# One-hots of Y for two buckets at once, eight of twelve one-hot rows on ScalarE, scaled tables and 120 columns in a graph tensor-product kernel

## The chip, the cores and the metric

The kernel runs on one core of a Trainium2 chip. The core has a matrix engine (TensorE: PE in the profile, its weight loads as PEld), an engine for elementwise work and reductions (VectorE, DVE), one for functions of single elements with a scale and a bias (ScalarE, ACT), a general engine (GpSimd, POOL), and SyncE (SP), which only issues transfers here. POOL also issues the indirect transfers, whose row numbers come from a tile. SBUF is the working memory of 128 partitions; PSUM takes the results of matmuls; HBM is the large memory. Each engine takes its instructions in the order of its own program, and semaphores order them between engines.

The metric is the device time of one execution in microseconds: 9987.23 us, the median of three runs (9973.58 to 9994.59).

## The reference

```python
N, deg, C, L, DE = 10000, 64, 64, 1, 4        # E = N * deg = 640000 edges, M = 4
R = _silu(edge_feat @ w_rad)                              # (E, C)
xs = x[src]                                               # (E, C, M)
tp = jnp.einsum('eci,ef,ifo->eco', xs, Y, cg)             # (E, C, M)
msg = R[:, :, None] * tp
agg = _segment_sum(msg.reshape(-1, C * M), dst, N).reshape(N, C, M)
return jnp.einsum('ncm,cd->ndm', agg, w_mix)
```

For each edge a row of 256 numbers of x is gathered, scaled per channel by R, combined with the edge's four numbers Y by a small tensor cg, summed over the edges with the same destination node, and mixed over the channels.

## The kernel before

**Sorting the edges.** The kernel sorts the edges by destination on the chip and then sums in each bucket of 32 nodes with matmuls. An edge travels as a row of W = 9 numbers: a tag (destination and source in one word), four of Y, four of edge_feat. The edges come in three parts (SPLIT). The first pass (`pass1`) sends a part's edges to NG = 20 groups of nodes; the second (`pass2`) sends a group's edges to its 15 or 16 buckets (297 + 16 = 313 buckets in all, 13 groups with 16 and 7 with 15). Both use `route`. A chunk is up to T tiles of 128 edges (T is 16 for the first pass of the first part, 24 elsewhere) and is handled as two pieces. For each tile, a matmul whose stationary operand is a one-hot of the row to which each edge goes (`onehots`, tile oh) and whose moving operand is the edges' words spread over slots (`spread`, tile X) puts the edges in place in PSUM (`move`, L585); `evict` copies the result to rt, and `store` (L604) writes it with an indirect transfer. The number of destination rows is Q = 120 in the first pass (20 groups with 6 rows each) and 128 in the second.

**One-hots.** In `onehots` DVE compares an iota with the row numbers for the first v rows of a piece (L569). ACT makes the last `self.act` rows: one Square for each row (L574, into the tile sq), which gives the squared distance, and one Relu over all of them (L575, from sq to oh), which turns 0 into 1 and the rest into 0. `act` is 3 in the first stage and 6 later; a full piece has 8 rows in the first stage and up to 12 later. In the first stage POOL makes the last `self.spare` = 3 tiles of X of each piece and DVE the rest (L557).

**Tables.** `tables` works out where each tile's edges start. Counts by a matmul (cnt), a copy out of PSUM on ACT into ps.cols (L437), a running sum on DVE with a floor `low` (L442), then the sums times B plus the bucket number (at, L456), split into two bf16 halves (sb, L458 and L459). From the totals n (L445) and a few small matmuls (prep, fo) come the row numbers of the stores; over and inc are repeated into ovr by two DVE copies (L471, L472). It is called 92 times: 6 + 26 for the first pass and 60 for the second.

**Messages.** `messages` goes over 939 units, one for each bucket and part, with 5 tiles of 128 edges in the first part and 6 in the others. At step k it runs, in four quarters, stages for units at some distance: `index` (8 ahead: source rows and destinations out of the tag), `gather` (5 ahead: one indirect transfer for each tile, on POOL, L866, into one of LG + 2 = 7 buffers xg), `fetch` (4 ahead: SP reads the sums of earlier parts back, L935, four buffers old), `turn` (2 ahead: a transpose on PE, L879), `sums` (0: 2 matmuls for each tile into the one PSUM buffer G, L921), `silu` (1 ahead: ACT, L892); `turned` (ACT, L884) and `spots` (1 ahead); `products` (1 ahead: DVE, x rows times R, L910) and `evict` (0: G plus old, on DVE, L950; in the first part a copy on ACT, L952); `radial` (2 ahead, PE, L889) and `full`. In `spots` DVE makes for one unit the one-hot of the node within the bucket (eq, in PSUM, L900) and multiplies it by the edge's four Y (S, L903, two buffers).

**Order.** In the first stage the first pass of the first part runs alone, with SP's order written out. After it `groups` weaves by hand the messages of a part with the second pass of the next group and the first pass of the next part; the orders of PE, DVE and ACT are those of the program, POOL's and SP's follow a planner. The last stage, from the third part's first message, has no first pass left in it.

## Time and profile before

| | |
|---|---|
| median of three runs | 9987.23 us |
| profiled execution | 9996.25 us, of which the span of the profile is 9994.5 us |
| granted TensorE clock, mean | 0.839 of full speed |
| transfers | 680358 packets, 1086.59 MB, 109 GB/s over the span |
| read from HBM, written | 855.28 MB, 222.79 MB |
| first gather of x rows of the three parts | 741.6, 3608.8 and 6861.4 us |
| last gather | 9849.1 us |

One execution is profiled. A row of a table of groups has the line of the kernel, the engine, the operation, the tiles out<-in with shapes and a count; behind the bar the busy time in us and the mean of one in ns; behind the second bar the engine's idle time just before these instructions and what ended it. "issue" means that the engine waited for nothing that the profile shows, "remote" that the releaser is not known. A row of a timeline begins with the start in us and the duration. The ends of matmuls are modelled.

### The profile page before, as it was taken

To read this page: it belongs to the slowest core of one execution; us is meant where nothing else is said; L and a number is where in the kernel's file an instruction comes from. 1 tells how busy PE (TensorE), PEld (TensorE's weight loads), DVE (VectorE), ACT (ScalarE), POOL (GpSimd) and SP (SyncE) were. 2 spreads that over 40 slices of the span, in tenths; PEclk is the share of its full clock that TensorE was granted. 3 is DMA by queue.
4 is the path that set the end of the run, shared out by engine and by line. 5 is a ranking of instruction groups with operands and counts; after the bars stand their busy time and mean duration, and the time that the engine had idled before them with its cause. 6 is when DMAs were issued, how large, how long until landed. Compare 5 with 4: busy or idle time off the path is not lost. (4 is left out here: it accounts for less than half of the span.)

```text
span 9994.5 us, 140280 instructions
## 1 busy us (share of the span) xinstructions
PE 7919.2 (79%) x49142; PEld 6708.4 (67%) x49142; DVE 6590.0 (66%) x11187; ACT 3711.5 (37%) x10488; POOL 5816.1 (58%) x6222
## 2 busy tenths in 40 slices
PE   7877888888887788888888888777778778787775
PEld 6766677777776667766666777666666666666654
DVE  7885777777775677777777777565555555555543
ACT  4763454445443343433333434222222222232210
POOL 3635555555556655665555566666666666666663
PEclk8987888888888888888888888878888888888887
DMA  6113333333333334443433444444333333333331
GB/s 238 43 38 102 108 103 99 105 103 101 105 104 107 107 107 118 117 122 110 117 110 111 116 119 115 125 120 121 109 108 112 110 107 109 110 110 108 111 109 55
DMA packets 680358, 1086.59 MB, mean 109 GB/s; under 512 B 255481, under 2 KB 484935, under 8 KB 673384
## 3 DMA queue, kind: packets, MB, share of 16 engines
q0 software_dynamic: 282224, 774.67, 27.5%
q1 hardware_dynamic: 396280, 295.24, 10.2%
q8 instruction: 390, 6.39, 0.3%
q10 hardware_dynamic: 1152, 7.74, 0.2%
q14 instruction: 312, 2.56, 0.1%
HBM read 855.28 MB, written 222.79 MB: 108 GB/s over the span
## 5 line engine op out<-in xcount | busy, mean ns | idle before, releaser
L866 POOL DMA_INDIRECT xg<-in_x_dram,sidx x5321 | 5079.1, 955 | 3288.4 <-issue 1397.8
L921 PE MATMUL G<-S,xg 128*128 128x128 f32 x21284 | 3159.1, 312 | 828.4 <-issue 323.0
L921 PEld LDWEIGHTS G<-S,xg 128*128 128x128 f32 x21284 | 3014.1, 226 | 933.6 <-issue 385.6
L585 PE MATMUL pr<-X,oh 128*128 128x81 f32 (+14 forms) x20530 | 2980.3, 303 | 670.5 <-issue 368.7
L585 PEld LDWEIGHTS pr<-X,oh 128*128 128x128 f32 x20530 | 2790.2, 211 | 871.4 <-issue 517.6
L910 DVE TENSOR_TENSOR xg<-xg,pre 128x1536 f32<-128x1536 f32 (+1 forms) x939 | 1557.2, 1658 | 457.2 <-ACT pre L892 318.1
L574 ACT ACTIVATE sq<-i,row 128x128 f32<-128x128 f32 x5322 | 1663.0, 391 | 18.9 <-DVE row L541 11.6
L557 DVE TENSOR_TENSOR X<-dv,Wt 128x2052 f32<-128x2052 f32 (+11 forms) x814 | 1336.8, 1642 | 453.6 <-remote 147.3
L892 ACT ACTIVATE pre<-pre 128x384 f32<-128x384 f32 (+1 forms) x939 | 430.2, 458 | 2918.9 <-remote 1284.2
L903 DVE TENSOR_TENSOR S<-dv,pay 128x768 f32<-128x768 f32 (+1 forms) x939 | 857.3, 913 | 232.9 <-remote 110.0
L889 PE MATMUL pre<-wr,sT 54*128 54x384 f32 (+1 forms) x1878 | 905.7, 564 | 86.5 <-ACT sT L884 47.3
L575 ACT ACTIVATE oh<-sq,ones 128x768 f32<-128x768 f32 (+1 forms) x1000 | 861.9, 862 | 102.0 <-PE pr L585 37.8
L950 DVE TENSOR_TENSOR Gs<-old,G 128x256 f32<-128x256 f32 x313 | 131.7, 421 | 1048.6 <-remote 536.6
L569 DVE TENSOR_TENSOR oh<-dv,row 128x768 f32<-128x768 f32 (+3 forms) x960 | 796.4, 833 | 8.4 <-PE pr L585 8.4
L524 ACT ACTIVATE pc<-pp 128x480 f32<-128x480 f32 (+8 forms) x500 | 234.9, 470 | 797.0 <-remote 210.1
L884 ACT ACTIVATE sT<-pre 54x128 f32<-54x128 f32 (+1 forms) x939 | 245.2, 261 | 579.8 <-remote 240.3
L889 PEld LDWEIGHTS pre<-wr,sT 54*128 54x128 f32 (+1 forms) x1878 | 302.6, 201 | 232.0 <-issue 97.5
L604 POOL DMA_INDIRECT grp<-rt,idx x240 | 277.0, 1154 | 305.7 <-ACT rt L595 119.6
L604 POOL DMA_INDIRECT bkt<-rt,idx x260 | 260.8, 1003 | 307.4 <-ACT rt L597 129.2
L879 PEld LDWEIGHTS pre<-ident,pay 128*54 128x54 f32 (+1 forms) x939 | 109.1, 116 | 481.3 <-issue 250.4
L950 DVE TENSOR_TENSOR Gp<-old,G 128x256 f32<-128x256 f32 x313 | 130.6, 417 | 449.3 <-remote 235.8
L879 PE MATMUL pre<-ident,pay 128*54 128x128 f32 (+1 forms) x939 | 293.2, 312 | 120.6 <-DVE xg L910 85.2
(259 smaller groups left out, 4791.5 us busy)
## 6 DMA issues: line engine op xcount, KB each, us to landing
xg<-in_x_dram,sidx POOLq DMA_INDIRECT x5321
sums<-Gp SPq DMA_DIRECT2D x626, 128.0 KB
old<-sums SPq DMA_DIRECT2D x626, 128.0 KB
bkt<-z SPq DMA_DIRECT2D x26, 1024.0 KB
grp<-z SPq DMA_DIRECT2D x16, 1024.0 KB
pay<-bkt SPq DMA_DIRECT2D x208, 54.0 KB
out_dram<-ot SPq DMA_DIRECT2D x69, 128.0 KB
grp<-z ACTq DMA_DIRECT2D x7, 1024.0 KB
```

The source lines that it names most:

```text
L557: eng.tensor_tensor(X[:, b:e], msk[:, b:e].unsqueeze(3).to_broadcast([P, e - b, w, W]), CH[c][1][:, a + b:a + e, :].unsqueeze(2).to_broadc ...
L569: nc.vector.tensor_tensor(oh[:, :v, :], self.v128.unsqueeze(1).to_broadcast([P, v, P]), row[:, a:a + v].unsqueeze(2).to_broadcast([P, v, P ...
L574: nc.scalar.activation(sq[:, u - v, :], self.i128, AF.Square, bias=row[:, a + u:a + u + 1], scale=-1.0)
L575: nc.scalar.activation(oh[:, v:m, :], sq[:, :m - v, :], AF.Relu, bias=self.ones[:, 0:1], scale=-2.0)
L585: nc.tensor.matmul(PR[c][:, ps.lo[t] * W:ps.hi[t] * W], oh[:, u, :], Xs[u], start=(t == 0), stop=(t == sizes[c] - 1), skip_group_check=True)
L604: nc.gpsimd.indirect_dma_start(out=ps.dst, out_offset=bass.IndirectOffsetOnAxis(ap=idx[:Q, i:i + 1], axis=0), in_=RT.pop(c), in_offset=None)
L866: nc.gpsimd.indirect_dma_start(out=xg[:, t, :], out_offset=None, in_=self.x, in_offset=bass.IndirectOffsetOnAxis(ap=si[:, u:u + 1], axis=0))
L889: nc.tensor.matmul(R, ST_.pop(k)[:ut * W], self.wr[:ut * W, :ut * 64], start=True, stop=True)
L892: nc.scalar.activation(RT[k], RT[k], AF.Silu)
L903: nc.vector.tensor_tensor(S[:, :ut], self.eq[:, :ut].unsqueeze(3).to_broadcast([P, ut, NB, 4]), pb[:, :, 1:5].unsqueeze(2).to_broadcast([P ...
L910: nc.vector.tensor_tensor(V, V, R.unsqueeze(3).to_broadcast([P, ut, 64, 4]), op=OP.mult)
L921: nc.tensor.matmul(G[:, h].rearrange("p n f -> p (n f)"), V[:, t, 32 * h:32 * h + 32, :].rearrange("p c i -> p (c i)"), S[:, t].rearrange( ...
```

## The change

- `pass_consts`: the floors `low` are multiplied by B and the bucket number is added once, at the start. In `tables` the counts leave PSUM with a scale of B. The running sum then is what `at` was: the scaling on DVE and the cast go, ACT copies the sums to sb in bf16, DVE subtracts as before. n is divided by B again, through an integer tile. The two copies into ovr move from DVE to ACT.
- `onehots`: oh is used with Q columns (120 in the first pass). ACT's squares are written into oh, and the Relu works in place; sq goes. `act` is 8 after the first stage. `move` writes Q rows.
- first stage: `spare` is 4: POOL makes four tiles of X of each piece.
- `pass1`: the tag's copy into the chunk (L707) moves from DVE to ACT.
- `spots`: every second bucket makes eq and S for two buckets in one instruction each; S has twice the size, still two buffers, and eq takes twice the place in PSUM. For that pay and dlc lie without gaps.
- `fetch`: 3 ahead and last in the step where it was 4 ahead and in the first quarter; three buffers old instead of four.

```diff
@@ pass_consts
+        for low in {id(p.low): p.low, id(p.last[0]): p.last[0]}.values():
+            low = low.rearrange("p (b t) -> p b t", b=B)
+            nc.vector.scalar_tensor_tensor(low, low, float(B), self.v128[:64, :B].unsqueeze(2).to_broadcast([64, B, T + 1]),
+                                           op0=OP.mult, op1=OP.add)
@@ tables
-        nc.scalar.activation(cols[:, :, 1:m + 1], cnt[:H, :m * B].rearrange("p (t b) -> p b t", b=B), AF.Copy)
+        nc.scalar.activation(cols[:, :, 1:m + 1], cnt[:H, :m * B].rearrange("p (t b) -> p b t", b=B), AF.Copy,
+                             scale=float(B))
...
-        n = w("n", B, 32)
-        nc.vector.tensor_copy(n[:N], sums[:N, :, m])
+        n, ni = w("n", B, 32), w("ni", B, 32, d=I32)
+        nc.vector.tensor_scalar(ni[:N], sums[:N, :, m], 1.0 / B, 0.5 / B - 0.5, op0=OP.mult, op1=OP.add)
+        nc.vector.tensor_copy(n[:N], ni[:N])
+        sb = wk.tile([H, ps.T * B], BF, name="sb", tag="sb" + ps.key, bufs=3)
+        tb = sb[:, :m * B].rearrange("p (t b) -> p b t", b=B)
+        nc.scalar.activation(tb, sums[:, :, :m], AF.Copy)
...
-        nc.vector.scalar_tensor_tensor(tb(at), sums[:, :, :m], float(B),
-                                       self.v128[:H, :B].unsqueeze(2).to_broadcast([H, B, m]), op0=OP.mult, op1=OP.add)
-        nc.vector.tensor_copy(sb[:, :m * B], at[:, :m * B])
-        nc.vector.tensor_tensor(sb[32:, :m * B], at[32:, :m * B], sb[32:, :m * B], op=OP.subtract)
+        nc.vector.tensor_tensor(tb[32:], sums[32:, :, :m], tb[32:], op=OP.subtract)
...
-        nc.vector.tensor_copy(two[:, 0], rep(over[:N, :B]))
-        nc.vector.tensor_copy(two[:, 1], rep(inc[:N]))
+        nc.scalar.activation(two[:, 0], rep(over[:N, :B]), AF.Copy)
+        nc.scalar.activation(two[:, 1], rep(inc[:N]), AF.Copy)
@@ onehots
-            oh = self.ph.tile([P, ps.H, P], F, name="oh", bufs=3)
+            oh = self.ph.tile([P, ps.H, P], F, name="oh", bufs=3)[:, :, :Q]
...
-            sq = self.ph.tile([P, self.act, P], F, name="sq", bufs=1)
             for u in range(v, m):
-                nc.scalar.activation(sq[:, u - v, :], self.i128, AF.Square, bias=row[:, a + u:a + u + 1], scale=-1.0)
-            nc.scalar.activation(oh[:, v:m, :], sq[:, :m - v, :], AF.Relu, bias=self.ones[:, 0:1], scale=-2.0)
+                nc.scalar.activation(oh[:, u], self.i128[:, :oh.shape[2]], AF.Square, bias=row[:, a + u:a + u + 1], scale=-1.0)
+            nc.scalar.activation(oh[:, v:m], oh[:, v:m], AF.Relu, bias=self.ones[:, 0:1], scale=-2.0)
@@ move
-                nc.tensor.matmul(PR[c][:, ps.lo[t] * W:ps.hi[t] * W], oh[:, u, :], Xs[u],
+                nc.tensor.matmul(PR[c][:Q, ps.lo[t] * W:ps.hi[t] * W], oh[:, u, :], Xs[u],
@@ pass1
-            nc.vector.tensor_copy(Wt[:, :m, 0].bitcast(I32), SB[b][:, o:o + m])
+            nc.scalar.activation(Wt[:, :m, 0], SB[b][:, o:o + m].bitcast(F), AF.Copy)
@@ messages
         def spots(k):
             g, j, s = units[k]
...
+            if j % 2:
+                return
+            ut = tiles(k)[1]
+            b = min(2, self.nb(g[1]) - j)
+            n = b * ut
+            pb = self.pay[g][:, j:j + b].rearrange("p b (t w) -> p (b t) w", w=W)
+            dl = IDX[g][1][:, j * ut:(j + b) * ut]
+            nc.vector.tensor_tensor(self.eq[:, :n], self.i32.unsqueeze(1).to_broadcast([P, n, NB]),
+                                    dl.unsqueeze(2).to_broadcast([P, n, NB]), op=OP.is_equal)
+            S = ph.tile([P, 2 * UT, NB, 4], F, name="S")
+            nc.vector.tensor_tensor(S[:, :n], self.eq[:, :n].unsqueeze(3).to_broadcast([P, n, NB, 4]),
+                                    pb[:, :, 1:5].unsqueeze(2).to_broadcast([P, n, NB, 4]), op=OP.mult)
+            for i in range(b):
+                SS[k + i] = S[:, i * ut:(i + 1) * ut]
...
-                OLD[g, j] = ph.tile([P, 2, 4, NB], F, name="old", bufs=4)
+                OLD[g, j] = ph.tile([P, 2, 4, NB], F, name="old", bufs=3)
...
-        quarters = (((index, LI), (gather, LG), (fetch, 4), (turn, 2), (sums, 0), (silu, 1)), ((turned, 2), (spots, 1)),
-                    ((products, 1), (evict, 0)), ((radial, 2), (full, -1)))
+        quarters = (((index, LI), (gather, LG), (turn, 2), (sums, 0), (silu, 1)), ((turned, 2), (spots, 1)),
+                    ((products, 1), (evict, 0)), ((radial, 2), (full, -1), (fetch, 3)))
@@ run
-            self.rt_bufs, self.ls, self.act, self.spare = 20, 10, 3, 3
+            self.rt_bufs, self.ls, self.act, self.spare = 20, 10, 3, 4
...
-            self.rt_bufs, self.ls, self.act, self.spare = 3, 4, 6, 0
+            self.rt_bufs, self.ls, self.act, self.spare = 3, 4, 8, 0
```

More of the change, by code (lines that the diff above doesn't have):

```diff
@@ L268, in consts @@
         self.vmsk = self.dv[:, P:]
-        self.eq = self.vmsk[:, :UT * NB].rearrange("p (t n) -> p t n", n=NB)
+        self.eq = self.vmsk[:, :2 * UT * NB].rearrange("p (t n) -> p t n", n=NB)
         d = iota("dif", [[1, P]], cm=-1, at=self.ph)
@@ L452, in tables @@
         nc.tensor.matmul(pre_p[0:1, 64:64 + B], self.ones[:N, 0:1], n[:N], start=True, stop=True)
-        at = wk.tile([64, ps.T * B], F, name="at", bufs=1)
-        sb = wk.tile([H, ps.T * B], BF, name="sb", tag="sb" + ps.key, bufs=3)
-        tb = lambda t: t[:, :m * B].rearrange("p (t b) -> p b t", b=B)
-        nc.vector.scalar_tensor_tensor(tb(at), sums[:, :, :m], float(B),
-                                       self.v128[:H, :B].unsqueeze(2).to_broadcast([H, B, m]), op0=OP.mult, op1=OP.add)
-        nc.vector.tensor_copy(sb[:, :m * B], at[:, :m * B])
-        nc.vector.tensor_tensor(sb[32:, :m * B], at[32:, :m * B], sb[32:, :m * B], op=OP.subtract)
+        nc.vector.tensor_tensor(tb[32:], sums[32:, :, :m], tb[32:], op=OP.subtract)
         yield
@@ L565, in onehots @@
             m = z - a
-            oh = self.ph.tile([P, ps.H, P], F, name="oh", bufs=3)
+            oh = self.ph.tile([P, ps.H, P], F, name="oh", bufs=3)[:, :, :Q]
             v = max(m - self.act, 0)
             if v:
-                nc.vector.tensor_tensor(oh[:, :v, :], self.v128.unsqueeze(1).to_broadcast([P, v, P]),
-                                        row[:, a:a + v].unsqueeze(2).to_broadcast([P, v, P]), op=OP.is_equal)
-            sq = self.ph.tile([P, self.act, P], F, name="sq", bufs=1)
+                nc.vector.tensor_tensor(oh[:, :v], self.v128[:, :Q].unsqueeze(1).to_broadcast([P, v, Q]),
+                                        row[:, a:a + v].unsqueeze(2).to_broadcast([P, v, Q]), op=OP.is_equal)
             for u in range(v, m):
-                nc.scalar.activation(sq[:, u - v, :], self.i128, AF.Square, bias=row[:, a + u:a + u + 1], scale=-1.0)
-            nc.scalar.activation(oh[:, v:m, :], sq[:, :m - v, :], AF.Relu, bias=self.ones[:, 0:1], scale=-2.0)
+                nc.scalar.activation(oh[:, u], self.i128[:, :oh.shape[2]], AF.Square, bias=row[:, a + u:a + u + 1], scale=-1.0)
+            nc.scalar.activation(oh[:, v:m], oh[:, v:m], AF.Relu, bias=self.ones[:, 0:1], scale=-2.0)
             XO[k][1] = oh
@@ L798, in pass2 @@
             n = sum(SPLIT[k][1])
-            pay = ph.tile([P, MB, max(sum(u) for _, u in SPLIT) * W], F, name="pay")[:, :, :n * W]
+            pay = ph.tile([P, MB * max(sum(u) for _, u in SPLIT) * W], F, name="pay")
+            pay = pay[:, :MB * n * W].rearrange("p (b q) -> p b q", b=MB)
             self.load_bucket(pay, k, g)
@@ L848, in index @@
             nc.vector.tensor_scalar(di[:, :m, :ut], key, 14, None, op0=OP.logical_shift_right)
-            dl = ph.tile([P, MB, MT], F, name="dlc", bufs=2)
+            dlc = ph.tile([P, MB * MT], F, name="dlc", bufs=2)[:, :m * ut]
+            dl = dlc.rearrange("p (b t) -> p b t", t=ut)
             n0, b, _ = self.grp[g[1]]
-            nc.vector.tensor_scalar(dl[:, :m, :ut], di[:, :m, :ut], float(TD), None, op0=OP.is_ge)
+            nc.vector.tensor_scalar(dl, di[:, :m, :ut], float(TD), None, op0=OP.is_ge)
             got = ph.tile([P, 1], F, name="got")
-            nc.vector.tensor_reduce(got, dl[:, :m, :ut], axis=AX.XY, op=OP.add)
+            nc.vector.tensor_reduce(got, dl, axis=AX.XY, op=OP.add)
             nc.vector.tensor_tensor(self.seen, self.seen, got, op=OP.add)
-            nc.vector.scalar_tensor_tensor(dl[:, :m, :ut], di[:, :m, :ut], -float(TD + n0),
+            nc.vector.scalar_tensor_tensor(dl, di[:, :m, :ut], -float(TD + n0),
                                            self.bn[b][:, :m].unsqueeze(2).to_broadcast([P, m, ut]),
                                            op0=OP.add, op1=OP.subtract)
-            IDX[g] = (si, dl)
+            IDX[g] = (si, dlc)
         def gather(k):
@@ L895, in spots @@
             g, j, s = units[k]
-            pb, ut = payload(k)
-            pb = pb.rearrange("p (t w) -> p t w", w=W)
-            t0 = tiles(k)[0]
-            dl = IDX[g][1][:, j, t0:t0 + ut]
-            nc.vector.tensor_tensor(self.eq[:, :ut], self.i32.unsqueeze(1).to_broadcast([P, ut, NB]),
-                                    dl.unsqueeze(2).to_broadcast([P, ut, NB]), op=OP.is_equal)
-            S = SS[k] = ph.tile([P, UT, NB, 4], F, name="S")
-            nc.vector.tensor_tensor(S[:, :ut], self.eq[:, :ut].unsqueeze(3).to_broadcast([P, ut, NB, 4]),
-                                    pb[:, :, 1:5].unsqueeze(2).to_broadcast([P, ut, NB, 4]), op=OP.mult)
+            if j % 2:
[12 more added lines that the diff above has]
+                SS[k + i] = S[:, i * ut:(i + 1) * ut]
         def products(k):
```

## The prediction

> **What bounds the kernel now.** I read the page's first lines, then the busy time by stage, then the waits of each engine in the long middle stages, then the timeline of one steady stretch of the first stage. The stages are cut where the first gather of x rows for each part of the edges starts (742, 3609 and 6861 us) and where the last one ends.

> ```profile
> span 9994.5 us, 140280 instructions
> PE 7919.2 (79%) x49142; PEld 6708.4 (67%) x49142; DVE 6590.0 (66%) x11187; ACT 3711.5 (37%) x10488; POOL 5816.1 (58%) x6222
> ```

> ```profile
> core 0: us, PE busy (x) PEld busy (x) DVE busy (x) ACT busy (x) POOL busy (x), PEclk, DMA share, GB/s
> 0.00:742.00 742.00, 588.44 (x4006) 506.76 (x4007) 612.00 (x1458) 464.76 (x1349) 317.26 (x486) 0.87 0.31 106
> 742.00:3609.00 2867.00, 2353.53 (x14949) 2012.86 (x14948) 2010.66 (x3374) 1305.47 (x3713) 1657.28 (x1722) 0.85 0.37 104
> 3609.00:6861.00 3252.00, 2633.98 (x16396) 2232.84 (x16397) 2286.50 (x3567) 1180.58 (x3253) 1947.71 (x2029) 0.84 0.42 117
> 6861.00:9850.00 2989.00, 2288.76 (x13535) 1915.84 (x13533) 1626.25 (x2597) 752.10 (x2143) 1876.80 (x1970) 0.83 0.39 110
> 7932.00:7936.00 4.00, 0.00 (x0) 0.00 (x0) 0.00 (x0) 0.00 (x0) 3.09 (x4) 0.78 0.38 107
> ```

> No engine is full. PE leads with 77 to 82% in the three long stages, DVE has 70% in the two middle ones (4297 of 6119 us) and 54% in the last, ACT 41% and 25%. PE, DVE and ACT each run in a hand-written order and hand work round, so the time is a chain that changes engine, most of it on PE. The last row shows another part of it: for 4 us PE, DVE and ACT all stand while the gathers go on. The waits of PE between 742 and 6861 us say who ends its pauses:

> ```profile
> PE pr L585 <- issue: 265.1, 378, 7.8
> PE G L921 <- issue: 218.3, 271, 3.9
> PE G L921 <- DVE Gp L950: 136.8, 35, 9.4
> PE G L921 <- ACT Gp L952: 89.3, 30, 7.8
> PE pr L585 <- ACT rt L595: 88.4, 32, 27.5
> PE pre L879 <- DVE xg L910: 82.4, 57, 6.6
> PE pr L585 <- DVE oh L569: 38.5, 21, 7.5
> DVE xg L910 <- ACT pre L892: 229.3, 72, 9.6
> ```

> The columns are microseconds in all, times, longest. PE is idle for 6119 - 4987.5 = 1131 us there. Of it 258 us end on DVE, at least 178 us on ACT, and 483 us on nothing that is shown. So PE bounds, and DVE ends about a quarter of PE's pauses.

> **The change part by part.** The forms that it touches:

> ```profile
> L569 DVE TENSOR_TENSOR oh<-dv,row 128x768 f32<-128x768 f32 x393 | 371.5, 948 | 0.0
> L569 DVE TENSOR_TENSOR oh<-dv,row 128x512 f32<-128x512 f32 x176 | 119.9, 681 | 0.0
> 8010.77 1.86 ACT L574 ACTIVATE sq<-i,row 128x128 f32<-128x128 f32 x6
> L575 ACT ACTIVATE oh<-sq,ones 128x768 f32<-128x768 f32 x774 | 723.8, 935 | 63.4 <-issue 34.4 <-PE pr L585 4.2 <-ACT sq L574 0.2
> L575 ACT ACTIVATE oh<-sq,ones 128x384 f32<-128x384 f32 x226 | 138.1, 611 | 38.6 <-PE pr L585 33.6 <-ACT sq L574 0.8
> L903 DVE TENSOR_TENSOR S<-dv,pay 128x768 f32<-128x768 f32 x626 | 599.2, 957 | 26.9 <-remote 5.4
> L903 DVE TENSOR_TENSOR S<-dv,pay 128x640 f32<-128x640 f32 x313 | 258.1, 825 | 206.0 <-remote 104.6 <-PE G L921 49.6 <-PE pre L879 14.9
> L900 DVE TENSOR_TENSOR dv<-dv,dlc 128x192 f32<-128x192 f32 x626 | 226.7, 362 | 8.7
> L900 DVE TENSOR_TENSOR dv<-dv,dlc 128x160 f32<-128x160 f32 x313 | 103.3, 330 | 5.2
> ```

> *One-hot rows of the routes.* After the first stage ScalarE makes 8 rows of a piece and DVE two fewer. DVE gains 948 - 681 = 267 ns a piece, on 774 pieces (the wide Relu's count): 206 us. ACT pays two squares at 1.86/6 = 0.31 us, and a Relu longer by 256 columns at (935 - 611)/384 = 0.84 ns, 0.22 us: 0.84 us a piece, 650 us in all. Writing the squares into oh adds no instruction; they now need the buffer that the Relu needed before, 0.3 to 2.5 us later. Its three buffers and the move one step behind cover that; the 37.8 us that Relus waited for PE (4.2 and 33.6) bound it.

> [...]

> *Spots for two buckets.* Of 939 pairs of instructions 480 stay (per part 13 groups of 16 buckets and 7 of 15). What goes is the fixed part: 957 - 768 x 1.03 = 166 ns and 362 - 192 x 1.0 = 170 ns by the slopes of the two forms; 459 x 336 ns = 154 us of DVE. The work comes in lumps: every other step DVE has about 1.0 us more ahead of the products and the evict, and 1.3 us less in the step between. I cost the lump at nothing against that relief; bounds plus and minus 40 us, the size of one such shift in a tenth of the steps. S has two buffers of two buckets, so the wait before S of 640 (206.0 us, mostly in the first part, for PE) mostly goes. PE was the late one there, so little comes home: -20 us, bounds 0 and -206.

> ```profile
> L456 DVE SCALAR_TENSOR_TENSOR at<-sums,dv 64x336 f32<-64x336 f32 (+7 forms) x92 | 76.5, 831 | 0.0
> L458 DVE CAST sb<-at 64x336 bf16<-64x336 f32 (+7 forms) x92 | 33.6, 366 | 3.0
> L472 DVE COPY ovr<-inc 4x128 f32<-4x128 f32 (+4 forms) x92 | 23.9, 260 | 0.1
> L463 ACT ACTIVATE f<-prep 4x128 f32<-4x128 f32 (+4 forms) x92 | 23.6, 257 | 171.9 <-remote 83.7 <-PE prep L452 45.9 <-issue 14.6
> L437 ACT ACTIVATE colsb<-cnt 64x336 f32<-64x336 f32 (+5 forms) x60 | 27.3, 455 | 70.8 <-PE cnt L431 35.8 <-remote 15.2 <-PE G L921 12.4
> L707 DVE COPY Wt<-si 128x24 int32<-128x24 int32 (+2 forms) x240 | 48.7, 206 | 42.5 <-POOL X L557 42.5
> L706 ACT ACTIVATE Wt<-es 128x96 f32<-128x96 f32 (+2 forms) x240 | 64.8, 273 | 0.0
> ```

> *Tables and tags.* DVE loses the scaling and the cast of the sums and the two copies into ovr (the second taken for both): 76.5 + 33.6 + 47.8 = 158 us, and gets one small conversion of n, about 92 x 0.2 = 18 us; 140 us less. ACT gets a copy like L437 and two like L463: 92 x (0.455 + 0.514) = 89 us. The tag copy moves: DVE -49, ACT 240 x 0.273 = 66 us.

> So DVE has 206 + 154 + 140 + 49 = 549 us less and ACT 805 us more. What arrives, by stage:

> Middle stages: 294 first-pass pieces and two thirds of the other 480, two thirds of the spots, some 66 of 92 tables, 147 tag copies: 164 + 103 + 100 + 30 = 397 us off DVE. It counts as far as DVE is on the chain. I take the quarter of PE's pauses that end on DVE: -100 us; bounds 0 and -397. ACT gets 614 x 0.84 + 66 x 0.97 + 147 x 0.27 = 620 us more and goes from 41 to 51%. It pays where DVE and PE wait for it. The rows show some 134 such waits (72 + 30 + 32); each later by a third of a one-hot block, 0.3 us, is +40 us; bounds 0 and 310, half of it.

> *120 columns.*

> ```profile
> L585 PEld LDWEIGHTS pr<-X,oh 128*128 128x128 f32 x20530 | 2790.2, 211 | 871.4 <-issue 517.6 <-ACT rt L595 112.6 <-DVE oh L569 84.4
> L879 PEld LDWEIGHTS pre<-ident,pay 128*54 128x54 f32 x626 | 69.7, 111 | 325.2 <-issue 170.5 <-DVE xg L910 81.1 <-DVE dv L900 9.8
> ```

> A weight load gets shorter by (211 - 111)/74 = 1.35 ns a column, 11 ns for 8. The 5000 tiles of the first pass load twice: 7000 loads after the first stage, 77 us at most; nothing where the matmul's own columns set the pace. About half the tiles have 126 or more of those, and part of PE's time is cover: -25 us.

> [...]

> *First stage.*

> ```profile
> 482.25 1.28 POOL L604 DMA_INDIRECT grp<-rt,idx  x1 [2.16 <-ACT oh L575]
> 483.57 0.95 POOL L557 TENSOR_TENSOR X<-msk,Wt 128x432 f32<-128x432 f32 x1
> 484.55 0.27 ACT L705 ACTIVATE Wt<-ys 128x64 f32<-128x64 f32 x1 [1.29 <-POOL X L557]
> 484.55 0.18 DVE L707 COPY Wt<-si 128x16 int32<-128x16 int32 x1 [1.53 <-POOL X L557]
> 494.63 0.18 DVE L707 COPY Wt<-si 128x16 int32<-128x16 int32 x1 [1.53 <-POOL X L557]
> ```

> Two chunks take 494.63 - 484.55 = 10.08 us, and in each such round DVE stands 1.53 us for POOL's X, which sat behind a store. The tag copy that stands there leaves DVE. DVE also has one X row less of a piece, 8 columns less of five one-hot rows, and no tag copies: about 1.1 us a round. POOL makes a fourth row, a third more of the 0.95 us: 0.3 us later, and ACT keeps its 1.29 us wait for it. With the shorter weight loads I take 0.75 us a round off 46 rounds: -35 us; bounds -75, and +15 if POOL's added time lands whole.

> *Last stage.* DVE -125 us, but its wait is for PE; -10 with ACT's share.

> *The fetch of old sums* is issued later, behind the evict of its own step, with three buffers.

> ```profile
> SPq L935 <- DVE Gp L950: 1072.1, 134, 20.5
> ```

> SP now stands at this fetch until DVE frees a buffer, so the lead is the depth: four buckets of about 9.7 us, then three, 29 us. Cost nothing, covered by that lead; were it short, each microsecond would come 626 times. SP's other loads behind it wait less, uncounted (bounds 0 and -30).

> The sum: -35 - 25 - 100 + 40 - 20 - 10 = -150 us against the profiled execution's own 9996.25 us (span 9994.5), which stands 9 us over the median 9987.23: **9837 us**.

> **The rivals.**
> *ScalarE comes late.* In program order the silu of the next bucket stands behind the one-hot block, which grows from 1.86 + 0.94 = 2.8 to 3.6 us; twice in a step where both passes run. DVE's products wait for silu (229.3 us already), PE for the products. Price: share s of 620 + 150 us. Break-even is s = (150 + 40)/770 = 25%; at 40% the time is 9987 - 190 + 308 = 10105 us. For it: ACT's work grows by 22%, and PE already waits 88.4 us for rt behind such blocks. Against: at 51% ACT has room, and its waits are mostly for PE.

> [...]

> *DVE is the bound in the middle.* Two thirds of the 397 us arrive and ACT costs nothing: 9987 - 35 - 25 - 265 - 20 - 10 = 9632 us. For it: 70% busy, and evict and products are DVE's. Against: PE's pauses name it for a quarter only.
> *PE's own pauses set the time.* The 483 us that end on nothing shown, and stretches like 7932 us, grow by what is saved, or pairs and fewer rows run but only in slack: 9987 - 35 - 25 + 40 = 9967 us, no change to speak of.

> **How the numbers follow.** Forecast 0.45, for 9740 to 9930; the strong DVE case 0.15, down to 9500; the case of PE's pauses 0.15, 9940 to 10010; late ScalarE 0.25, 10010 to 10250. Within 0.2% (20 us) is about what a measurement of this kernel cannot tell from no change. Faster: 0.45 + 0.15 + 0.06 = 0.66; same: 0.09; slower: 0.25. The range 9600 to 10100 leaves out about 0.07 below and 0.12 above.

> **What would show it.** Right: oh on DVE at 681 and 548 ns where it was 948 and 812, S at some 1.75 us x480; DVE busy near 6000 us, ACT near 4500; PE's waits for Gp and xg shorter; 9.3 us rounds in the first stage; the middle stages 100 us shorter. Wrong: waits of DVE's xg on ACT's pre well over 350 us, PE waiting for oh on ACT, evicts that wait for old, or a first stage that waits longer for POOL.

## The result and the profile after

The changed kernel takes 10060.11 us, the median of five runs (10055.84 to 10090.54), against 9975.12 us of the kernel before (five runs, 9958.10 to 9994.59) on the same chip. The ratio is 1.0076, with an interval of 1.0060 to 1.0092: slower by some 85 us, where 150 us less were forecast. The profiled execution took 10090.54 us, with a span of 10088.8.

The page's first lines of the changed kernel, then its busy time by stage, cut in the same places as before (first gather of each part at 765.0, 3681.4 and 6970.5 us, last gather at 9938.5); the columns are those of the table of before:

```profile
span 10088.8 us, 140287 instructions
PE 7970.2 (79%) x49142; PEld 6743.6 (67%) x49142; DVE 6280.3 (62%) x9757; ACT 4489.3 (44%) x12552; POOL 5881.8 (58%) x6222
```

```profile
0.00:765.00 765.00, 585.83 (x4000) 500.74 (x4001) 634.86 (x1323) 484.73 (x1530) 343.76 (x486) 0.85 0.29 103
765.00:3681.40 2916.40, 2406.18 (x14958) 2058.26 (x14957) 1879.74 (x2906) 1614.61 (x4513) 1671.68 (x1721) 0.83 0.35 102
3681.40:6970.50 3289.10, 2642.24 (x16401) 2232.90 (x16400) 2157.02 (x3103) 1476.40 (x3997) 1967.22 (x2030) 0.83 0.40 115
6970.50:9938.50 2968.00, 2277.60 (x13527) 1908.77 (x13525) 1555.58 (x2241) 904.99 (x2482) 1881.17 (x1968) 0.83 0.38 111
```

By stage the span grew by 23, 49 and 37 us and shrank by 21 in the last; the tail is 6 us longer. In the two middle stages PE makes the same 31,000 matmuls, with 6692 of the routes' weight loads at 120 columns (210 ns each, the rest 218; all 213 at 128 columns before), and is busy for 5048.4 us where it was 4987.5; its idle time went from 1131 to 1157 us. So of 87 us lost there 61 are busy time for the same matmuls, beside a granted clock that fell from 0.85 and 0.84 to 0.83. What is left, 26 us, is waiting. DVE did get less work (-310 us of busy time), ACT more (+778).

The waits in the two middle stages:

```profile
PE pr L587 <- issue: 249.7, 329, 5.6
PE G L930 <- DVE Gp L959: 112.3, 33, 9.2
PE pr L587 <- ACT rt L597: 105.3, 43, 5.4
PE pre L883 <- DVE xg L919: 64.6, 42, 5.4
PE pr L587 <- ACT oh L577: 56.2, 33, 8.1
DVE xg L919 <- ACT pre L896: 399.2, 96, 11.0
DVE X L560 <- PE pr L587: 251.3, 88, 9.3
```

PE waits less for DVE, as forecast (Gp 112.3 after 136.8, xg 64.6 after 82.4), and more for ACT: rt, the copy that empties the PSUM of the routes, 105.3 after 88.4, and its one-hots 56.2, which were a small wait before:

```profile
PE pr L585 <- ACT oh L575: 24.9, 12, 7.8
```

DVE now stands 399.2 us for silu (229.3). The groups that the change touched:

```profile
L572 DVE TENSOR_TENSOR oh<-dv,row 128x480 f32<-128x480 f32 (+5 forms) x960 | 572.8, 601 | 1.9 <-PE pr L587 0.9 <-ACT pc L527 0.8
L910 DVE TENSOR_TENSOR S<-dv,pay 128x1536 f32<-128x1536 f32 (+1 forms) x480 | 785.2, 1636 | 23.9 <-issue 2.0 <-PE G L930 1.6
L907 DVE TENSOR_TENSOR dv<-dv,dlc 128x384 f32<-128x384 f32 (+1 forms) x480 | 254.9, 531 | 7.8
L454 ACT ACTIVATE sb<-sums 64x336 bf16<-64x336 f32 (+7 forms) x92 | 171.3, 1862 | 115.7 <-DVE sums L447 69.0 <-issue 27.7 <-DVE Gp L959 16.5
L462 DVE TENSOR_TENSOR sb<-sums,sb 32x336 bf16<-32x336 f32 (+7 forms) x92 | 166.8, 1813 | 72.1 <-ACT sb L454 44.3 <-issue 25.0 <-ACT Wt L709 1.3
```

One-hots on DVE fell by 224 us (206 in the sum) and the pairs by 72.1 + 75.1 = 147 us (154), so these were sized well. The tables were not: ACT's copy of the sums takes 1.86 us, the mean over its shapes, where the sum had 0.455, and DVE's subtraction, which I had not priced at all, went from 0.56 to 1.81 us. It was this before:

```profile
L459 DVE TENSOR_TENSOR sb<-at,sb 32x336 bf16<-32x336 f32 (+7 forms) x92 | 51.1, 556 | 3.1
```

Both now write bf16 with a step from element to element, where before only the fp32 tile at was written so. The cast on DVE shows the same: 0.98 us with that step (run 11), 0.37 without it in the kernel before (L458). That is 129 us more on ACT than counted, and 116 us more on DVE.

In the first stage the timeline shows the rounds of two chunks that were forecast, and one thing that was not:

```profile
484.93 0.26 ACT L707 ACTIVATE Wt<-ys 128x64 f32<-128x64 f32 x1 [0.91 <-POOL X L560]
...
485.79 0.96 POOL L560 TENSOR_TENSOR X<-msk,Wt 128x432 f32<-128x432 f32 x1
486.02 1.20 DVE L560 TENSOR_TENSOR X<-msk,Wt 128x432 f32<-128x432 f32 x1
...
491.37 0.59 DVE L560 TENSOR_TENSOR X<-msk,Wt 128x432 f32<-128x432 f32 x1
...
494.22 0.26 ACT L707 ACTIVATE Wt<-ys 128x64 f32<-128x64 f32 x1 [0.86 <-POOL X L560]
```

A round takes 494.22 - 484.93 = 9.29 us (10.08 before). But DVE's X of 128x432 takes 1.20 us while POOL makes its own, and 0.59 alone. So DVE, with a row less in each piece, is busy longer with X in the first stage than before (the first row is of before):

```profile
L557 DVE TENSOR_TENSOR X<-msk,Wt 128x540 f32<-128x540 f32 (+1 forms) x186 | 185.6, 1000 | 29.7 <-ACT Wt L706 29.7
L560 DVE TENSOR_TENSOR X<-msk,Wt 128x432 f32<-128x432 f32 (+1 forms) x186 | 211.8, 1141 | 41.5 <-ACT Wt L708 40.7 <-PE pr L587 0.8
```

### The profile page after: what moved, and what is told of

It is laid out like the page before. It is cut to its first block, busy times and chain, and to the rows that moved or that the text cites. A ratio compares the mean times of both kernels' runs of the same rounds, so it can differ in the third digit from the quotient of the medians.

```text
span 10088.8 us, 140287 instructions
## 1 busy us (share of the span) xinstructions
PE 7970.2 (79%) x49142; PEld 6743.6 (67%) x49142; DVE 6280.3 (62%) x9757; ACT 4489.3 (44%) x12552; POOL 5881.8 (58%) x6222
## 5 line engine op out<-in xcount | busy, mean ns | idle before, releaser
L930 PE MATMUL G<-S,xg 128*128 128x128 f32 x21284 | 3182.8, 313 | 792.1 <-issue 329.1
L587 PE MATMUL pr<-X,oh 128*128 128x108 f32 (+20 forms) x20530 | 3008.0, 305 | 741.3 <-issue 350.4
L587 PEld LDWEIGHTS pr<-X,oh 128*120 128x120 f32 (+1 forms) x20530 | 2807.4, 212 | 949.0 <-issue 506.7
L576 ACT ACTIVATE oh<-i,row 128x128 f32<-128x128 f32 (+1 forms) x6870 | 2087.9, 388 | 69.7 <-PE pr L587 52.3
L577 ACT ACTIVATE oh<-oh,ones 128x1024 f32<-128x1024 f32 (+3 forms) x1000 | 1007.2, 1007 | 38.1 <-remote 10.4
L910 DVE TENSOR_TENSOR S<-dv,pay 128x1536 f32<-128x1536 f32 (+1 forms) x480 | 785.2, 1636 | 23.9 <-issue 2.0
L572 DVE TENSOR_TENSOR oh<-dv,row 128x480 f32<-128x480 f32 (+5 forms) x960 | 572.8, 601 | 1.9 <-PE pr L587 0.9
```

The lines of the kernel that those rows point to most:

```text
L572: nc.vector.tensor_tensor(oh[:, :v], self.v128[:, :Q].unsqueeze(1).to_broadcast([P, v, Q]), row[:, a:a + v].unsqueeze(2).to_broadcast([P, ...
L576: nc.scalar.activation(oh[:, u], self.i128[:, :oh.shape[2]], AF.Square, bias=row[:, a + u:a + u + 1], scale=-1.0)
L577: nc.scalar.activation(oh[:, v:m], oh[:, v:m], AF.Relu, bias=self.ones[:, 0:1], scale=-2.0)
L587: nc.tensor.matmul(PR[c][:Q, ps.lo[t] * W:ps.hi[t] * W], oh[:, u, :], Xs[u], start=(t == 0), stop=(t == sizes[c] - 1), skip_group_check=True)
L910: nc.vector.tensor_tensor(S[:, :n], self.eq[:, :n].unsqueeze(3).to_broadcast([P, n, NB, 4]), pb[:, :, 1:5].unsqueeze(2).to_broadcast([P, n ...
L930: nc.tensor.matmul(G[:, h].rearrange("p n f -> p (n f)"), V[:, t, 32 * h:32 * h + 32, :].rearrange("p c i -> p (c i)"), S[:, t].rearrange( ...
```

## The experiments

The ratios below are to the kernel before on the same chip, with 95% intervals. The chips differ: the kernel before took 8254 us on that of the first four runs and 9985 to 10135 us on the others.

**Four parts taken back, one at a time.** The theories were: A, ScalarE is late; B, the pairs clump PE's pauses; C, the tables' hops; D, POOL's X against DVE's in the first stage.

```diff
# 1: six rows
-            self.rt_bufs, self.ls, self.act, self.spare = 3, 4, 8, 0
+            self.rt_bufs, self.ls, self.act, self.spare = 3, 4, 6, 0
# 2: the edits of eq, pay, dlc and spots undone
# 3: table instructions on VectorE
-        nc.scalar.activation(tb, sums[:, :, :m], AF.Copy)
+        nc.vector.tensor_copy(tb, sums[:, :, :m])
-        nc.scalar.activation(two[:, 0], rep(over[:N, :B]), AF.Copy)
-        nc.scalar.activation(two[:, 1], rep(inc[:N]), AF.Copy)
+        nc.vector.tensor_copy(two[:, 0], rep(over[:N, :B]))
+        nc.vector.tensor_copy(two[:, 1], rep(inc[:N]))
# 4: spare = 3, and the tag's copy on VectorE
```

> The changed kernel with 6 instead of 8 one-hot rows on ScalarE after the first stage (squares still in place, everything else of the change kept). Theory A (ScalarE is late: its longer blocks put off silu, the copies of rt and its own one-hots, and the clock falls with the longer pauses of PE): 9960 us or less against 10060, granted clock back at 0.84, DVE's waits of xg for pre back near 230 us in the middle stages. Theory B (pairs of spots clump PE's pauses): within 20 us of 10060, since DVE gets 200 us of work back. Theory C (tables): within 20 us of 10060.

> The changed kernel with eq and S made for one bucket at a time again. Theory A: 10060 or up to 30 us more, DVE some 150 us busier. Theory B (every second step DVE has 1 us more ahead of the products, so PE's pauses become fewer and longer, and a longer pause costs clock as well): 9980 us, the count of PE's pauses over 2 us falls from 251 towards 199, clock 0.838. Theory C: 10060.

> The changed kernel with three ScalarE instructions of each table (the bf16 copy of the sums, two copies into ovr) on VectorE again; the scaled floors and counts stay. Theory A: 10040, a small part of ScalarE's added work (some 70 of 775 us) goes. Theory B: 10060. Theory C (each table's chain got hops between DVE and ScalarE, and PE stands at fo, pr and pp for it): 9990, with the first gather of x rows back from 765 to about 742 us.

> The changed kernel with three X tiles of each piece on GpSimd in the first stage and the tag's copy on VectorE, as before. Theory D (the first stage's loss of 23 us comes from GpSimd's and VectorE's X running against each other, 1.20 us a 128x432 tile instead of 0.6 to 0.7): first gather back near 742 us, 10035 us in all. If D falls: first gather at 765 us or later and 10060 to 10090 us, since the steady rounds go back from 9.3 to 10.1 us. Theories A and B say nothing of the first stage; the tag's copies after it give ScalarE 40 us back, so 10050 by A.

Measured: 1.0041 (1.0028 to 1.0053), 1.0180 (1.0167 to 1.0194), 1.0183 (1.0168 to 1.0199) and 1.0223 (1.0210 to 1.0237). The absolute numbers expected were those of the other chip. The three kernels that keep 8 rows stand 1.4 to 1.8% above the one with 6, which is theory A. B and C fall as main causes: with the pairs or the tables taken back the kernel is still 1.8% slower than before. D falls too: run 4 has its first gather at 768.3 us, later than runs 2 and 3 (760.9 and 752.7), and takes 0.4% longer. The changed kernel itself was not run on this chip, so what each of these parts is worth cannot be read from these four.

**The changed kernel as an anchor, the one-hot part alone, and the fetch.** The second is the kernel before with the edits of `onehots` and `move` alone, `act` still 6; the third is the changed kernel with

```diff
-        quarters = (((index, LI), (gather, LG), (turn, 2), (sums, 0), (silu, 1)), ((turned, 2), (spots, 1)),
-                    ((products, 1), (evict, 0)), ((radial, 2), (full, -1), (fetch, 3)))
+        quarters = (((index, LI), (gather, LG), (fetch, 4), (turn, 2), (sums, 0), (silu, 1)), ((turned, 2), (spots, 1)),
+                    ((products, 1), (evict, 0)), ((radial, 2), (full, -1)))
```

> The changed kernel itself on the chip of this group of runs, as the anchor for the others: the kernel before took 8254 us on the chip of the last group against 9975, so ratios are compared. All theories: slower than before by 0.8 to 2%; if two one-hot rows on ScalarE are the main loss, some 1.3% above the run with 6 rows on ScalarE, that is 1.017 of before.

> The kernel before with the one-hot part alone, and 6 rows on ScalarE as before: squares written into oh and the Relu in place, 120 columns in the first pass. [...] Rival: squares in place wait for oh's buffer until PE has read it (ScalarE stands in front of PE), and the time is 1.002 to 1.005 of before, which would be the rest of the loss that the run with 6 rows showed.

> The changed kernel with the fetch of old sums 4 ahead and in the first quarter again, still three buffers: SP then stands at the fetch longer, for a buffer that comes free a step later. Prediction's term for the fetch is nothing: same as the changed kernel within 0.15%. Rival (old sums land late for the evict since the fetch was put later): 0.3 to 0.5% faster than the changed kernel.

Measured: 1.0068 (1.0046 to 1.0090), 0.9992 (0.9978 to 1.0006) and 1.0094 (1.0072 to 1.0117). Squares in place and 120 columns change nothing that can be told, and the fetch at its old place is no faster, 13 us slower with overlapping intervals: its cost of nothing was right. The one-hot part with the pairs and nothing else (run 7) gave no time: its tiles need 184.7 KB of a partition where 182.2 are left. So the pairs are priced by taking them back, in runs 2 and 12.

**The two rows alone, and what is left without them.** The first is the one-hot part with one line more; the second is run 1 again, the third adds the edit of run 3 to it, the fourth that of run 2 as well.

```diff
-            self.rt_bufs, self.ls, self.act, self.spare = 3, 4, 6, 0
+            self.rt_bufs, self.ls, self.act, self.spare = 3, 4, 8, 0
```

> The kernel before with the one-hot part alone (in place, 120 columns) and 8 rows on ScalarE after the first stage; the same without the two added rows was 0.9992 of before. Theory A (the two rows carry the loss): 1.006 to 1.012 of before, DVE's waits of xg for pre up as in the changed kernel, most of it in the first of the two middle stages. Rival (the loss is in ScalarE's other added work and the two rows only pay together with it): 0.999 to 1.002.

> The changed kernel with 6 rows on ScalarE, run a second time, since the chips of the two groups of runs so far differ (8254 and 9985 us for the kernel before) and the changed kernel itself was on one of them alone. Theory A: 1.000 to 1.004 of before, against 1.007 for the changed kernel on a chip where before takes 9985 us, and against 1.017 on one where it takes 8254.

> The changed kernel with 6 rows on ScalarE and the three table instructions on VectorE again. If the tables' hops to ScalarE are the rest of the loss: 0.4% faster than the run with 6 rows alone, at or under before (0.996 to 1.000), first gather some 8 us earlier. If the rest is in the pairs or the fetch: within 0.1% of the run with 6 rows alone.

> The run before this one with spots for one bucket at a time again; what is left of the change are the one-hots in place with 120 columns, the scaled floors, the first stage and the later fetch. If pairs clump PE's pauses: 0.2 to 0.5% faster than the run before this one. Prediction's term (154 us of VectorE come back): up to 0.3% slower.

Measured: 1.0111 (1.0092 to 1.0130), 0.9944 (0.9925 to 0.9964), 0.9928 (0.9909 to 0.9947) and 0.9947 (0.9931 to 0.9964). The first and the one-hot part with 6 rows (0.9992) were on two chips, where the kernel before takes 9999 and 9985 us. Two rows by themselves cost 1.2%, more than the whole change. Without them the change gains 56 us on this chip, more than theory A expected, and 72 with the tables on DVE. The pairs are worth some 24 us, with intervals that overlap. So the other parts do help, and the two rows take that and more.

How they cost it stands in the clocks and first lines of the one-hot part with 6 rows:

```profile
core 0: 9953.0 us, clock 0.840
```

```profile
PE 7845.9 (79%) x49142; PEld 6649.2 (67%) x49142; DVE 6566.3 (66%) x11187; ACT 3662.6 (37%) x10488; POOL 5803.4 (58%) x6222
```

and with 8:

```profile
core 0: 10110.0 us, clock 0.831
```

```profile
PE 7958.1 (79%) x49142; PEld 6737.6 (67%) x49142; DVE 6369.2 (63%) x11187; ACT 4264.9 (42%) x12036; POOL 5802.8 (57%) x6222
```

Of 157 us between the two profiles, 112 are PE's busy time, for the same 49142 matmuls; 45 are idle. (The ratios give 119 us: the first profile is the fastest of its twelve executions, and the chips are 14 us apart.) The lower mean clock alone would make some 85 of the 112, an estimate from 7845.9 x 0.840 / 0.831. Now the waits from 760 to 6900 us, with 6 rows:

```profile
PE pr L584 <- ACT rt L594: 82.6, 31, 27.6
PE pr L584 <- ACT oh L574: 14.3, 6, 7.9
DVE xg L909 <- ACT pre L891: 247.4, 75, 10.7
DVE X L557 <- PE pr L584: 113.1, 50, 7.9
```

and with 8:

```profile
PE pr L584 <- ACT rt L594: 118.0, 41, 26.7
PE pr L584 <- ACT oh L574: 59.9, 37, 6.8
DVE xg L909 <- ACT pre L891: 223.2, 74, 9.8
DVE X L557 <- PE pr L584: 245.4, 82, 9.3
```

PE's routing matmuls wait for ACT in two places, for one-hots (46 us more) and for rt (35 us more); and DVE, which needs an X buffer that these matmuls still hold, stands behind PE. The wait for silu, which the prediction and theory A had named, does not grow with the two rows. Inside the whole change the two rows show mostly in the one-hots. With 6 rows (run 10) the two waits of PE are these, where the changed kernel has 105.3 and 56.2:

```profile
PE pr L587 <- ACT rt L597: 100.9, 36, 26.5
PE pr L587 <- ACT oh L577: 20.7, 14, 5.7
```

**Late one-hots, or what stands behind them?** The first two keep 6 rows and DVE's share and add three squares to each piece after the first stage, behind the Relu or ahead of the squares; they write a tile that nobody reads. The third has 8 rows, the fourth is run 11 with `act` = 4.

```diff
# 13, behind the Relu (14: ahead of the squares)
+            if self.act == 6:
+                sx = self.ph.tile([P, P], F, name="sx", bufs=1)
+                for u in range(3):
+                    nc.scalar.activation(sx, self.i128, AF.Square, bias=row[:, a:a + 1], scale=-1.0)
# 15
                 spread(k)
+                onehots(k)
             yield HALF if 0 <= k < NP + lag else 1
-            if 0 <= k < NP:
-                onehots(k)
```

> The kernel before with the one-hot part alone (6 rows on ScalarE, 0.9992 of before) and three squares of 0.31 us into a spare tile behind the Relu of each piece after the first stage: 0.93 us, a little more than the 0.84 us that the two rows add, without making the one-hots late. If the loss comes from what stands behind the block on ScalarE (silu, the copies of rt, the evicts): 1.010 to 1.012 of before, as with 8 rows. If it comes from the one-hots themselves arriving late at PE: 0.999 to 1.003.

> The same three squares ahead of the squares of the rows, so that the one-hots of each piece are late by 0.93 us as well as all that stands behind them; VectorE keeps its rows. If the one-hots themselves arrive late: 1.010 to 1.014 of before, clearly over the run with the squares behind. If what stands behind the block carries the loss: the same as that run within 0.15%.

> The one-hot part with 8 rows on ScalarE (1.0111 of before), the whole block issued half a step earlier, right behind the spread of its piece. If late one-hots are the loss: 1.000 to 1.005, since they get several microseconds of lead back. If ScalarE's work behind the block is the loss: 1.008 to 1.015, the block only stands before other work.

> The changed kernel with the table instructions on VectorE again and 4 rows on ScalarE instead of 6 (0.9928 of before) or 8. If each row on ScalarE costs as the seventh and eighth did (0.6% a row): 0.981 of before. If the price starts where ScalarE's block outlasts VectorE's share of the step: 0.991 to 0.999, VectorE now 200 us busier.

Measured: 1.0118 (1.0097 to 1.0139), 1.0166 (1.0145 to 1.0187), 1.0041 (1.0023 to 1.0058) and 0.9909 (0.9891 to 0.9927). Squares that delay no one-hot of their own piece cost 1.26% over the 0.9992 without them, as much as the two rows; ahead of the rows they cost 0.48% more. But they were not of the same length as the rows: ACT is busy for 4541.3 us in run 13, 879 more than the 3662.6 without the squares, where the two rows add 602, and DVE keeps its rows. By ACT's time, in us of the kernel for each us of ACT, the squares behind cost about 0.14, ahead 0.20, and the two rows 0.20: an estimate across three chips. So of what the squares cost some 70% goes with what stands behind the block on ACT, and the rest with the one-hots' own delay. The waits of the run with the squares behind:

```profile
PE pr L588 <- ACT rt L598: 158.6, 45, 27.8
PE pr L588 <- ACT oh L574: 12.9, 7, 4.4
DVE xg L913 <- ACT pre L895: 262.6, 82, 9.6
DVE X L557 <- PE pr L588: 220.1, 71, 14.4
```

Here the one-hots are hardly waited for, and rt is, twice as long as without the squares (82.6), with the same stand of DVE behind it: with the squares, rt is what comes late. With two real rows it is rt and the one-hots, and how the price divides between them in the changed kernel was not settled. The block of 8 rows half a step earlier costs 0.7% less, which by the numbers expected spoke for late one-hots, and both waits are shorter there (rt 94.4 us, one-hots 31.0); against the two runs with squares it says only that the place counts as well as the length, and how it does stays open. With 4 rows the time is as with 6 or a little less, so the fifth and sixth row do not cost the 0.6% each of the seventh and eighth.

**Place or length.** Both at the earlier place, with the tables on VectorE; the third is run 16 again.

> The changed kernel with 6 rows on ScalarE, the table instructions on VectorE (0.9928 of before) and the one-hot block half a step earlier. If the earlier place is better for a block of any length: 0.988 to 0.991. If it only repairs a block that is too long: 0.992 to 0.996.

> The same with 4 rows on ScalarE (0.9909 at the later place). If rt behind the block is what is paid, a short block costs little at either place: 0.989 to 0.993. Earlier one-hots on VectorE stand ahead of spots and products there: up to 0.995 if that decides.

> The run with 4 rows on ScalarE and the tables on VectorE a second time, as the anchor for the two others: 0.989 to 0.993 of before.

Measured: 0.9930 (0.9917 to 0.9943), 0.9952 (0.9940 to 0.9965) and 0.9892 (0.9878 to 0.9907). The earlier place only repairs a block that is too long: with 6 rows it changes nothing (0.9928 at the later place), with 4 it is worse. The version with 4 rows and the table instructions on VectorE is about 1% faster than the kernel before in both of its runs (10029.97 against 10124.43 us, 10024.21 against 10135.03), and so beats both kernels.

## Why the prediction was wrong

- *One-hot rows.* This is the step that failed: "each later by a third of a one-hot block, 0.3 us, is +40 us". I counted the waits for ACT that were there and made each a little longer. The two rows alone cost 119 us (1.0111 against 0.9992), with DVE's gain already in; on ACT they are 4264.9 - 3662.6 = 602 us. That is a share of 20% where 40 of 620 us, 6%, was taken. In its place the runs show new waits of PE, for the one-hots (14.3 to 59.9 us) and for rt behind the block (82.6 to 118.0), and a lower clock (0.840 to 0.831), with 112 us more of PE's busy time against 45 of idle time.
- *DVE's work as a quarter.* "PE's pauses that end on DVE: -100 us" was too much for this part: the rows' 197 us on DVE show as no gain beside that loss. For the pairs it was nearer: 154 us brought some 24, a sixth. DVE also lost only 310 of the 549 us of busy time that the sum took off it: the tables' subtraction took back 116, X in the first stage 26.
- *The late rival* had the right sign and the right engine, but not the path. It went through silu, which the two rows do not make later; rt, which it named in passing, and the one-hots are what PE waits for. Its condition was too strict as well: it asked for a share of 25%, and about 20% decided, as the other gains came to some 56 us instead of 190. The two rows take 602 us of ACT where they took 197 of DVE, both in fp32, but what the runs show of the loss is who waits for ACT. The sign that I named for the case, DVE's wait for pre well over 350 us, did appear (399.2 us), and is no sign of it: run 10, without the two rows, is faster than before and has 399.6 us. That wait came with the pairs, as run 12 without and run 11 with them show; the third row is run 10:

```profile
DVE xg L912 <- ACT pre L894: 264.5, 78, 9.4
DVE xg L919 <- ACT pre L896: 368.4, 99, 11.0
DVE xg L919 <- ACT pre L896: 399.6, 106, 12.0
```

  The other sign of a wrong forecast, PE waiting for oh on ACT, is the one that follows the two rows.

- *Tables.* The duration of the copy was taken from a row of another layout. With the three instructions on DVE the kernel gains 16 us more, within the intervals.
- *120 columns* were put at -25 us: the one-hot part alone came to 0.9992, between 22 us faster and 6 slower. That leaves out the 25 us narrowly. That the matmul's own columns set the pace for about half the tiles was my estimate, which no run shows by itself. The loads did get shorter, by 59 us in all (PEld 6649.2 after 6708.4), but the time did not follow.
- *First stage.* The forecast rounds are there, the 35 us are not. Counted in the trace, the first forty stores came 23 us later (362.2 instead of 339.4 us), the next 53 took 18 us less, and the way from there to the first gather grew by 19 us. The last part goes with the two rows and the tables: without them the first gather is at 748.1 us (run 11). The sum also took a gain from DVE's X, which got 26 us longer instead. Yet with both the fourth X tile of POOL and the tag's copy on ACT taken back (run 4) the fortieth store still comes at 352.3 us, so they explain less than half of the late start, and the rest stays open.
- *S buffers, fetch and last stage* came about as forecast: DVE's wait before S went from 233 to 24 us (what that brought was not measured by itself), the fetch costs nothing, the last stage is 21 us shorter where 10 were counted.

## What to carry to other kernels

An engine that is 40% busy is not free (ACT was busy for 37% of the span in run 6, and two rows more cost 1.2%): what decides is what stands behind the new instructions in its order, and who waits for that. A moved block can be priced ahead by adding idle instructions at its place, which needs one run; measure their length in the trace, for here they came out nearly half longer than the block. With the two rows 112 of the 157 us between the profiles were busy time for the same matmuls, at a mean clock of 0.831 after 0.840. As I read the counts below, a pause of PE cost twice here, once as a wait and again as slower work after it, so busy time at the granted clock belongs into the sum.

## What the runs showed of the hardware

```profile
4083.52:4086.93 3.41, 2.23 (x15) 1.80 (x16) 3.21 (x9) 1.68 (x6) 2.56 (x3) 1.00 0.27 77
4086.93:4090.34 3.41, 3.41 (x18) 3.41 (x18) 3.24 (x8) 3.34 (x9) 2.74 (x3) 0.50 0.64 181
4117.65:4121.06 3.41, 0.82 (x3) 0.56 (x3) 3.34 (x3) 2.36 (x6) 1.98 (x2) 1.00 0.35 97
4121.06:4124.48 3.42, 2.90 (x9) 1.85 (x8) 3.35 (x7) 0.00 (x0) 1.92 (x2) 0.50 0.25 75
```

After a stretch in which PE was busy 2.23 of 3.41 us, the next runs at half clock, in which 18 matmuls fit, where 15 had run in the 2.23 us. Counted over the whole trace, 74% of the 442 stretches with 1 to 2 us of idle PE and all of the 415 with more than 2 us are followed by one at half clock, and 9% of the 1456 with none (0.02 us at most). Of stretches that are themselves at full clock it is 62% of 297, all of 210 and 0.5% of 963. These are counts of what follows on what; no run changed the pauses alone.

Chips differ. On the chip of runs 1 to 4 the kernel before takes 8254 us, 17% less. (Each chip was measured in one group of runs, so that it is the chip and not the hour is not shown.) The page of run 1 there, against the changed kernel:

```profile
L930 PE MATMUL G<-S,xg 128*128 128x128 f32 x21284 | 2898.3, 299 | 71.3 <-ACT Gp L961 28.7
```

```profile
L930 PE MATMUL G<-S,xg 128*128 128x128 f32 x21284 | 3182.8, 313 | 792.1 <-issue 329.1
```

The pauses that end on nothing shown, the largest group of PE's waits on the other chips (350.4 us before pr and 329.1 before G in the changed kernel), hardly exist there (1.9 us before G in run 1, and none listed before pr). What makes them was not found. The two rows cost some 1.4% there, judged by runs 2 and 3, which lack the pairs or the tables, and 1.2% on the others; but the version with 6 rows, 0.6% faster than the kernel before elsewhere, is 0.4% slower there. The version with 4 rows was not run on it.
